# Attention and a SwiGLU FFN on one core: the result tiles of an output group dealt out differently, and two batches of VectorE work issued one instruction per TensorE step

## The chip, the cores and the metric

The kernel runs on one core of a Trainium2 chip. The metric is the device time of one execution in microseconds; the median of three runs of the kernel before is 1584.55 us. Engines are called as the profile calls them: PE (TensorE matmul), PEld (its weight loads), DVE (VectorE), ACT (ScalarE), POOL (GpSimd), SP (the queue that issues the DMAs).

## The reference

```python
# q, k, v: (8, 12, 448, 64) float32
q_n, k_n = rmsnorm(q, g_q), rmsnorm(k, g_k)
scores = q_n @ k_n.T / sqrt(64)                    # per sequence and head
attn = exp(scores - max) / (sum + 1e-9)
x = (attn @ v) as (B*S, H*D)                       # (3584, 768)
xn = x / rms(x) * rms_g
g = xn @ w_gate;  val = xn @ w_val                 # (768, 1536) each
out = (silu(g) * val) @ w_out                      # (1536, 768)
```

## The kernel before

Eight sequences (b = 0 to 7) of 448 tokens go through two halves. The attention half works in 48 groups g of two heads; six groups make a sequence. The FFN half of earlier sequences is laid between the attention's matmuls as a list of small **steps**: in the steady part, while the attention of one sequence runs, the gate and value products of the sequence before it run, and the output projection of the one before that. Everything is float32.

The order is written out by hand. `pe(fn)` emits one step of PE work, counts a clock `now["t"]` by one, and then emits whatever `after(n, ...)` has made due at that count, in the order in which it was asked for. `fill()` takes FFN steps from the list `todo`, calls `pe` for each, and behind each may emit one small DVE job more. An engine runs its own instructions in the order of emission; between engines, semaphores hold an instruction until its data, and the place it writes, are ready. A pool with a few buffers gives them out in the order in which they were released.

**Gate and value products.** `quad(b, fp)` (fp = 0 to 5) works out one block with seven half-size products (`p1`, `p6`, `p2`, `p7`, `p5`, `p4`, `p3_last`). `product` is line 1000. The result of `p1` is copied by ACT from its PSUM bank to the SBUF tile `p1` (line 1044), since `p2` goes on adding onto that same bank. The partial sums u2, u3, c21 and cc are DVE adds (line 1012) into single-buffer tiles of these names. `hand` (lines 1019 to 1023) makes h = silu(gate) * value.

**Output projection in quads.** For b = 2, 3, 5, 6, 7 (`in_quads`) the output projection is `out_quads`: a Strassen scheme within a Strassen scheme. There are seven groups i = 0 to 6 (`ORDER_Q`: B11, B21, T2, T3, T4, T1, B22), each of four steps: `a`, `bb`, `c` (12 PE records each) and `d` (6 records), with `d(i)` emitted after `a(i + 1)`. All their matmuls are line 1296. `c(i)` ends in one DVE add out of its bank (line 1328); `d(i)` accumulates onto one half of the same bank and so waits for that add; its own add is line 1335. `left_q1` (line 1171) makes the left operands of group i+1 by three DVE instructions within `c(i)`, and a fourth within `bb`. A group's result sits in two 128x384 places `dst[i]`, given by `rows(name)`: some in tiles of the `quad` code (p1, c21, u2, u3, cc), some in output tiles y. `finish(i)` combines groups on POOL (line 1268): after T1 it adds T1 onto `dst[3]`, then T2 (`dst[2]`) onto T1; after B22, the last group, it adds T1 (`dst[5]`) onto B22.

**The two seams.** Where a quad projection ends, the first product `p1` of the next gate block is emitted ahead of the last `d(6)`, and its ACT copy is put one step later, behind `d(6)`. I call this the **closing seam**; it exists at b = 3, 4, 6, 7.

Where a gate block ends and its output projection begins is the **opening seam**. Count steps from `p3_last` of fp = 5 as step 0. Step 1 is `norm_x` of the next sequence (a PE transposition that spreads 1/rms; for the last sequence an empty step), then come `a(0)`, `bb(0)`, `c(0)`, `a(1)`, `d(0)`, `bb(1)`, `c(1)`, `a(2)`, `d(1)`, `bb(2)` and so on, with attention steps between in most places. Into these steps fall three batches of DVE work:

- six scalings of x (`scale`, line 663, in place), two each at steps 1, 2 and 3;
- two times four **left sums** of the outer scheme (`left_sums`, lines 1148 to 1151), four at step 3 and four at step 4; the first group that reads one is i = 2;
- four sums of the scaled x (`op`, line 680, the list `slow`), one behind each FFN step once three steps have gone by since `norm_x`, if the group's attention steps are four steps back. `p1` of the next block empties what is left.

Of the kernel before, what the change touches and what calls it, by code (L numbers as in the profile page):

```python
# [8 lines left out]
F32 = mybir.dt.float32  # L9
# [3 lines left out]
ALU = mybir.AluOpType  # L13
# [5 lines left out]
B, H, S, D = 8, 12, 448, 64  # L19
# [3 lines left out]
NPAIR = H // 2  # L23
NDC, NFC = DM // 128, DF // 128
HALF = DM // 2
BW = 384
# [309 lines left out]
def safe_scores(  # L336
# [20 lines left out]
    nc = tc.nc  # L357
# [7 lines left out]
    e_pool, tmp, y_pool, rest_pool = pool("c_e", 11), pool("c_tmp", 1), pool("c_y", 3), pool("c_rest", 2)  # L365
# [8 lines left out]
    st = {}  # L374


    now, due = {"t": 0}, []

    def after(n, fn):
        due.append((now["t"] + n, fn))  # L380
# [6 lines left out]
            item[1]()  # L387


    NG = B * NPAIR  # L390


# [258 lines left out]
    def norm_x(b):  # L651


        rs = st.pop(("rx", b))
        ps = (ps_s if b else ps_f).tile([128, 512], F32, name="rb", tag="s" if b else "f")
        for t in range(NT):
            nc.tensor.transpose(ps[:, t * P:(t + 1) * P], rs[:, t:t + 1].to_broadcast([P, 128]), ident[0:P, 0:P])

        xs = [st["x", b, h] for h in range(2)]

        def scale(hp):
            x = xs[hp // 3][:, hp % 3, :]
            nc.vector.scalar_tensor_tensor(x, x, rg[:, hp:hp + 1], ps[:, 0:S], ALU.mult, ALU.mult)  # L663

        for hp in range(NPAIR):
            if b:
                after(hp // 2, lambda hp=hp: scale(hp))
            else:
                scale(hp)
        if b == 0:  # L670
            return

        a = st["left", b] = {f"A{r + 1}{h + 1}": xs[h][:, :, r * HT:(r + 1) * HT] for r in range(2) for h in range(2)}
        for h in range(2):
            st.pop(("x", b, h))

        def op(name, first, second, what):

            a[name] = a["A21"] if name == "S3" else s_pool.tile([128, 3, HT], F32, name="xs")
            nc.vector.tensor_tensor(a[name], a[first], a[second], what)  # L680

        slow.extend(lambda args=args: op(*args) for args in (("S1", "A21", "A22", ALU.add), ("S2", "S1", "A11", ALU.subtract),
                                                             ("S3", "A11", "A21", ALU.subtract), ("S4", "A12", "S2", ALU.subtract)))
        st["x_at"] = now["t"]

    slow = []

    def hurry():
        while slow:
            slow.pop(0)()  # L690

    NFP = NFC // 2

# [80 lines left out]
    for fc in range(NFC):  # L774
        col, fp = divmod(fc, NFP)
# [66 lines left out]
    def in_quads(b):  # L842
        return b > 1 and len(out_pairs(b)) == 2
# [161 lines left out]
    def quad(b, fp):  # L1005

        bank, add = {}, {}
        shift = 64 * (b % 2)

        def plus(name, ps, other, dst=None):  # L1010
            add[name] = tmp.tile([128, S], F32, name=name, tag=name, bufs=1) if dst is None else dst
            nc.vector.tensor_tensor(add[name], ps[:, 0:S], add[other], ALU.add)  # L1012

        def hand(gate, value, dst):

            th = tmp.tile([128, S], F32, name="th", tag="th", bufs=2)
            n = gate.shape[-1] * (gate.shape[1] if len(gate.shape) == 3 else 1)
            th = th[:, 0:n] if len(gate.shape) == 2 else th.rearrange("p (r n) -> p r n", r=2)
            nc.scalar.activation(th, gate, ACT.Tanh, scale=0.5)  # L1019

            def rest():
                nc.vector.scalar_tensor_tensor(dst, th, 1.0, gate, ALU.add, ALU.mult)
                nc.vector.scalar_tensor_tensor(dst, dst, 0.5, value, ALU.mult, ALU.mult)

            after(1, rest)

        def rows(fc):
            return h_of(fc)[:, shift:shift + S]

        def p1():  # L1030
            if fp == 0:
                hurry()
            if fp < 2:

                for g in (fp, fp + 2):
                    if carries(b - 1):
                        nc.gpsimd.tensor_copy(carried[g], group(out_pairs(b - 1)[-1][1] + 1, g))
                    if b % 2:
                        nc.gpsimd.tensor_copy(hs[g][:, :, 0:64], hs[g][:, :, S - 64:S])
            bank["a"] = product(b, fp, "A11", "B11")  # L1040

            def copy():
                add["p1"] = tmp.tile([128, S], F32, name="p1", tag="p1", bufs=1)
                nc.scalar.copy(add["p1"], bank["a"][:, 0:S])  # L1044

            if fp == 0 and in_quads(b - 1):
                after(1, copy)
            else:
                copy()

        def p6():
            bank["b"] = product(b, fp, "S2", "T2")
            plus("u2", bank["b"], "p1")

        def p2():
            product(b, fp, "A12", "B21", onto=bank["a"])
            hand(bank["a"][:, 0:HT], bank["a"][:, HT:S], rows(fp)[:, 0:HT])

        def p7():
            bank["c"] = product(b, fp, "S3", "T3")  # L1060
            plus("u3", bank["c"], "u2")

        def p5():
            bank["e"] = product(b, fp, "S1", "T1")
            add["cc"] = tmp.tile([128, 2, S], F32, name="cc", tag="cc", bufs=1)
            plus("c22", bank["e"], "u3", dst=add["cc"][:, 1, :])

        def p4():
            bank["d"] = product(b, fp, "A22", "T4")
            plus("c21", bank["d"], "u3")  # L1070
            after(1, lambda: hand(add["c21"][:, 0:HT], add["c21"][:, HT:S], rows(fp)[:, HT:S]))

        def p3():
            product(b, fp, "S4", "B22", onto=bank["e"])
            plus("c12", bank["e"], "u2", dst=add["cc"][:, 0, :])
            after(1, lambda: hand(add["cc"][:, :, 0:HT], add["cc"][:, :, HT:S], rows(fp + NFP).rearrange("p (r n) -> p r n", r=2)))

        def sums(n):

            st["left_sums"] = now["t"]  # L1080
            half = fp // KG
            if n < len(out_pairs(b)):
                left_sums(b, n, half)

        def p3_last():
            if fp == NFP - 1 and in_quads(b):
                after(1, lambda: left_q1(b, 0, range(3)))
            p3()
            if fp % KG == KG - 1:
                after(3, lambda: sums(0))  # L1090
                after(4 if fp == NFP - 1 else 5, lambda: sums(1))

        return [p1, p6, p2, p7, p5, p4, p3_last]

    OUT_PARTS = 3
# [45 lines left out]
    def left_sums(b, n, half):  # L1141

        pair, row = (0, n) if in_quads(b) else (n, 0)
        if half == 0:
            for i, name in enumerate(("S1", "S2", "S4")):
                st["so", b, pair, row, name] = room_so[3 * n + i].rearrange("p (c n) -> p c n", c=NFP)
        of = lambda name: left_group(b, pair, name, row, half)
        nc.vector.tensor_tensor(of("S1"), of("A21"), of("A22"), ALU.add)
        nc.vector.tensor_tensor(of("S2"), of("S1"), of("A11"), ALU.subtract)
        nc.vector.tensor_tensor(of("S3"), of("A11"), of("A21"), ALU.subtract)  # L1150
        nc.vector.tensor_tensor(of("S4"), of("A12"), of("S2"), ALU.subtract)

    def left_o(b, pair, name, c):
        return left_group(b, pair, name, 0, c // KG)[:, c % KG, :]
# [88 lines left out]
    def out_quads(b):  # L1243

        bank, dst, steps = {}, {}, []
# [5 lines left out]
        def rows(name):  # L1251

            if name in ("B11", "T1"):
                return [tmp.tile([128, S], F32, name=t, tag=t, bufs=1)[:, 0:BW] for t in ("p1", "c21")]
            if name == "T3":
                u3 = tmp.tile([128, 2, S], F32, name="cc", tag="cc", bufs=1)
                return [u3[:, row, 0:BW] for row in range(2)]
            if name == "T2":
                return [tmp.tile([128, S], F32, name=t, tag=t, bufs=1)[:, 0:BW] for t in ("u2", "u3")]
            return [y_pool.tile([128, HALF], F32, name="y", tag="y") for _ in range(2)]  # L1260

        def out(what, n, first):
# [62 lines left out]
        def c(i):  # L1325
            ps = two(i, "c")
            u3 = st["u", b, i][:, 1:2].to_broadcast([128, 2, HW])
            nc.vector.tensor_tensor(dst[i][1].rearrange("p (h n) -> p h n", h=2), ps, u3, ALU.add)  # L1328
            if i + 1 < len(ORDER_Q):
                left_q1(b, i + 1, range(3))  # L1330

# [63 lines left out]
    def fill(n=None):  # L1395
# [8 lines left out]
        for _ in range(min(n, len(todo))):  # L1404
# [10 lines left out]
            pe(fn)  # L1415
            convert()

            if slow and now["t"] - st["block"] > 4 and now["t"] - st["x_at"] > NPAIR // 2:
                slow.pop(0)()
            if now["t"] - st["block"] > 4 and now["t"] != st.get("left_sums"):  # L1420
                left = 3 - sum(derive() for _ in range(3))
# [77 lines left out]
        for _ in range(n):  # L1499
            convert()  # L1500


    def at_once(steps):
        for step in steps:
            step()

    at_once(squares(0, 0))
    warm(9)
# [1 line left out]
    scale = norm_rests(0, 0, 2)  # L1510
    steps = squares(0, 1)
# [11 lines left out]
    for g in range(NG + 1):  # L1523
        b, hp = divmod(g, NPAIR)
# [124 lines left out]
```

## Time and profile before

| | |
|---|---|
| median of 3 runs | 1584.55 us (1583.27 to 1585.42) |
| the profiled execution: its own time | 1584.46 us |
| its span, first to last instruction | 1582.7 us |
| PE busy | 1546.3 us, 98% of the span |
| DVE busy | 978.9 us, 62% |
| POOL busy | 723.8 us, 46% |
| ACT busy | 473.3 us, 30% |
| mean granted PE clock | 0.995 |
| opening seams, start of `a(0)` | about 624, 818, 1182, 1373 and 1523 us |
| closing seams, end of the last group | about 694, 888, 1254 and 1432 us |

A row of a group or of the timeline reads: start, duration, engine, line and operation, output from input as partitions x elements, the number of instructions, and in brackets the idle time ahead of it with the instruction that ended it. A PE row counts hardware records, two for each matmul in the code. In the table of waits the three numbers are the total, the number of times and the longest, in us.

### The profile page before, as it was taken

To read this page: it belongs to the slowest core of one execution; us is meant where nothing else is said; L and a number is where in the kernel's file an instruction comes from. 1 tells how busy PE (TensorE), PEld (TensorE's weight loads), DVE (VectorE), ACT (ScalarE), POOL (GpSimd) and SP (SyncE) were. 2 spreads that over 40 slices of the span, in tenths; PEclk is the share of its full clock that TensorE was granted. 3 is DMA by queue.
4 is the path that set the end of the run, shared out by engine and by line. 5 is a ranking of instruction groups with operands and counts; after the bars stand their busy time and mean duration, and the time that the engine had idled before them with its cause. 6 is when DMAs were issued, how large, how long until landed. Compare 5 with 4: busy or idle time off the path is not lost.

```text
span 1582.7 us, 23667 instructions
## 1 busy us (share of the span) xinstructions
PE 1546.3 (98%) x7916; PEld 1195.9 (76%) x7916; DVE 978.9 (62%) x1697; ACT 473.3 (30%) x955; POOL 723.8 (46%) x718
## 2 busy tenths in 40 slices
PE   8999999999999999999999999999999999999997
PEld 4344445787756888788878888667887788899997
DVE  6889898669754666854567444534658545563454
ACT  6746464232222222223222222323322222101000
POOL 6867877454324443564335652444544541021003
PEclk9999999999999999999999999999999999999998
DMA  7648574866789979785547854584557744578565
GB/s 209 211 144 265 165 242 138 264 215 214 246 274 290 316 221 300 225 259 154 160 141 243 250 158 140 154 265 131 160 152 224 232 143 143 159 246 259 174 194 185
DMA packets 313414, 327.10 MB, mean 207 GB/s; under 512 B 83652, under 2 KB 310212, under 8 KB 313284
## 3 DMA queue, kind: packets, MB, share of 16 engines
q1 hardware_dynamic: 312356, 325.30, 66.6%
q8 instruction: 65, 1.06, 0.3%
q14 instruction: 65, 0.53, 0.1%
q10 hardware_dynamic: 800, 0.20, 0.1%
q0 software_dynamic: 128, 0.00, 0.0%
HBM read 271.62 MB, written 53.77 MB: 206 GB/s over the span
## 4 chain that ended last, share of the span: by engine, by line
PE 72%; DVE 12%; issue 1%; POOL 1%; DMA 1%; ACT 0%; SPq 0%; DVEq 0%; POOLq 0%
PE ff L1000 40%; PE ff L1296 9%; PE ff L1228 5%; PE sc L545 5%; PE av L597 5%; PE ff L1104 2%; PE sc L575 2%; DVE l L1171 2%; PE den L610 2%; PE tr L527 1%; DVE rd L618 1%; DVE x L663 1%; DVE top L768 1%; DVE top L769 1%; DVE ms L487 0%
## 5 line engine op out<-in xcount | busy, mean ns | idle before, releaser
L1000 PE MATMUL ff<-x,w 128*128 128x224 f32 x1866 | 380.9, 354 | 4.0 <-ACT p L1044 4.0
L1000 PEld LDWEIGHTS ff<-x,w 128*128 128x128 f32 x1866 | 348.2, 190 | 20.8 <-issue 11.1
L555 POOL TENSOR_TENSOR es<-e 128x448 f32<-128x448 f32 x82 | 93.1, 1156 | 437.3 <-ACT e L549 437.3
L1000 PE MATMUL ff<-xs,w 128*128 128x224 f32 x1392 | 284.6, 353 | 3.2 <-DVE w L922 2.9
L1000 PEld LDWEIGHTS ff<-xs,w 128*128 128x128 f32 x1392 | 261.9, 190 | 4.9 <-issue 4.1
L562 POOL TENSOR_TENSOR es<-es,e 64x448 f32<-64x448 f32 (+1 forms) x164 | 196.4, 1208 | 6.3
L618 DVE RECIPROCAL rd<-rd 128x448 f32<-128x448 f32 x41 | 121.0, 2951 | 94.4 <-ACT rd L617 94.4
L549 ACT ACTIVATE e<-sc,rs 128x448 f32<-128x448 f32 x288 | 161.5, 635 | 49.8 <-PE sc L545 47.4
L545 PE MATMUL sc<-qT,kT 64*128 64x448 f32 x576 | 138.0, 572 | 1.9 <-ACT e L549 0.7
L597 PE MATMUL av<-e,vt 128*64 128x448 f32 x576 | 118.8, 548 | 0.0
L506 POOL TENSOR_TENSOR rs<-ms,mhalf 128x12 f32<-128x12 f32 (+1 forms) x50 | 115.9, 2318 | 4.2
L545 PEld LDWEIGHTS sc<-qT,kT 64*128 64x128 f32 x576 | 54.0, 185 | 82.5 <-issue 68.5
L1296 PE MATMUL ff<-w,l 128*128 128x192 f32 x578 | 110.9, 332 | 4.7 <-DVE c L1328 3.6
L1012 DVE TENSOR_TENSOR cc<-ff,u 128x448 f32<-128x448 f32 x84 | 52.4, 624 | 100.9 <-PE ff L1000 100.8
L1361 PE MATMUL ff<-x,w 128*128 128x448 f32 x288 | 111.8, 542 | 0.0
L1296 PEld LDWEIGHTS ff<-w,l 128*128 128x128 f32 x578 | 97.5, 193 | 8.7 <-DVE c L1328 4.2
L597 PEld LDWEIGHTS av<-e,vt 128*64 128x64 f32 x576 | 37.1, 136 | 75.6 <-issue 74.8
L1361 PEld LDWEIGHTS ff<-x,w 128*128 128x128 f32 x288 | 53.3, 190 | 50.7 <-issue 48.9
L1019 ACT ACTIVATE th<-c 128x224 f32<-128x224 f32 x42 | 16.3, 389 | 227.1 <-DVE c L1012 227.1
L1268 POOL TENSOR_TENSOR y<-y,p 128x384 f32<-128x384 f32 x10 | 11.6, 1160 | 154.4 <-DVE y L1335 150.3
L631 POOL TENSOR_TENSOR ss<-ss,rd 128x448 f32<-128x448 f32 x40 | 46.4, 1159 | 77.2 <-ACT rd L630 77.2
L809 POOL TENSOR_TENSOR w<-top,raw 128x384 int32<-128x384 int32 x63 | 66.4, 1068 | 25.9 <-issue 8.4
(201 smaller groups left out, 2335.0 us busy)
## 6 DMA issues: line engine op xcount, KB each, us to landing
w<-kept SPq DMA_DIRECT2D x512, 192.0 KB, 3.5
w<-kept_q SPq DMA_DIRECT2D x323, 192.0 KB, 3.5
w<-kept_o SPq DMA_DIRECT2D x136, 192.0 KB, 3.8
kept<-w SPq DMA_DIRECT2D x91, 192.0 KB, 3.7
kept_q<-w SPq DMA_DIRECT2D x57, 192.0 KB, 3.2
qk<-in_q_dram SPq DMA_DIRECT2D x48, 192.0 KB, 3.7
qk<-in_k_dram SPq DMA_DIRECT2D x96, 96.0 KB, 3.6
vt<-in_v_dram SPq DMA_DIRECT2D x48, 192.0 KB, 3.5
```

Of the source, the lines that this page charges most:

```text
L506: nc.gpsimd.tensor_tensor(st["rs", g][:, cols], ms, mhalf[:, cols], ALU.pow)
L545: nc.tensor.matmul(ps[:, 0:S], lhsT=kT[r, c * 128:(c + 1) * 128], rhs=qT[r, :], start=True, stop=True)
L549: nc.scalar.activation(e, ps[:, 0:S], ACT.Exp, scale=rs[:, n:n + 1])
L555: nc.gpsimd.tensor_tensor(es, st["e", g, 0, j], st["e", g, 1, j], ALU.add)
L562: nc.gpsimd.tensor_tensor(es[r], es[r], e[r], ALU.add)
L597: nc.tensor.matmul(av[own(j), 0:S], lhsT=vt[:, j, c], rhs=st["e", g, c, j], start=False, stop=(c == NK - 1), skip_group_check=True)
L618: nc.vector.reciprocal(rd, rd)
L809: nc.gpsimd.tensor_tensor(data(key).bitcast(I32), top, lo, ALU.add)
L1000: nc.tensor.matmul(bank[:, w * HT:(w + 1) * HT], lhsT=wt[:, c * 128:(c + 1) * 128], rhs=x[:, c, :], start=onto is None and w == c == 0, st ...
L1228: nc.tensor.matmul(ps, lhsT=left_o(b, which, LEFT_O[name], c), rhs=data(("wo", b, name, c)), start=first and c == 0, stop=c == NFP - 1, sk ...
L1296: nc.tensor.matmul(ps, lhsT=a[:, j, :], rhs=data(key)[:, n % 2 * HW:(n % 2 + 1) * HW], start=start and j == 0, stop=j == KG - 1, skip_grou ...
L1361: nc.tensor.matmul(bank[w][:, 0:S], lhsT=data(key)[:, c * 128:(c + 1) * 128], rhs=st["x", 0, half][:, c, :], start=half == c == 0, stop=ha ...
```

## The change

Five edits:

1. **Places.** `rows` gives groups B11 and T1 the tiles (c21, u3) in place of (p1, c21), and T2 the tiles (p1, u2) in place of (u2, u3).
2. **The copy of p1** is emitted within `p1` everywhere; the special case that moved it behind `d(6)` is gone.
3. **Left sums.** For quad blocks the second half's eight sums are put on a list `first_sums` at step 3. `fill` emits one behind each FFN step, and `c(1)` empties the list before it makes the left operands of group 2. For other blocks, all sums of the last fp come at step 3.
4. **Scaling of x** goes one per step, at steps 1 to 6.
5. **The sums of x** (`slow`) begin once six steps have gone by since `norm_x`, and only when `first_sums` is empty.

```diff
             if b:
-                after(hp // 2, lambda hp=hp: scale(hp))
+                after(hp, lambda hp=hp: scale(hp))
...
-    slow = []
-
-    def hurry():
-        while slow:
-            slow.pop(0)()
+    slow, first_sums = [], []
+
+    def hurry(jobs):
+        while jobs:
+            jobs.pop(0)()
...
             bank["a"] = product(b, fp, "A11", "B11")
-
-            def copy():
-                add["p1"] = tmp.tile([128, S], F32, name="p1", tag="p1", bufs=1)
-                nc.scalar.copy(add["p1"], bank["a"][:, 0:S])
-
-            if fp == 0 and in_quads(b - 1):
-                after(1, copy)
-            else:
-                copy()
+            add["p1"] = tmp.tile([128, S], F32, name="p1", tag="p1", bufs=1)
+            nc.scalar.copy(add["p1"], bank["a"][:, 0:S])
...
                 after(3, lambda: sums(0))
-                after(4 if fp == NFP - 1 else 5, lambda: sums(1))
+                after(3 if fp == NFP - 1 else 5, lambda: sums(1))
...
-        nc.vector.tensor_tensor(of("S1"), of("A21"), of("A22"), ALU.add)
-        nc.vector.tensor_tensor(of("S2"), of("S1"), of("A11"), ALU.subtract)
-        nc.vector.tensor_tensor(of("S3"), of("A11"), of("A21"), ALU.subtract)
-        nc.vector.tensor_tensor(of("S4"), of("A12"), of("S2"), ALU.subtract)
+        ops = [lambda args=args: nc.vector.tensor_tensor(*(of(name) for name in args[:3]), args[3])
+               for args in (("S1", "A21", "A22", ALU.add), ("S2", "S1", "A11", ALU.subtract),
+                            ("S3", "A11", "A21", ALU.subtract), ("S4", "A12", "S2", ALU.subtract))]
+        if half and in_quads(b):
+            first_sums.extend(ops)
+        else:
+            at_once(ops)
...
             if name in ("B11", "T1"):
-                return [tmp.tile([128, S], F32, name=t, tag=t, bufs=1)[:, 0:BW] for t in ("p1", "c21")]
+                return [tmp.tile([128, S], F32, name=t, tag=t, bufs=1)[:, 0:BW] for t in ("c21", "u3")]
...
             if name == "T2":
-                return [tmp.tile([128, S], F32, name=t, tag=t, bufs=1)[:, 0:BW] for t in ("u2", "u3")]
+                return [tmp.tile([128, S], F32, name=t, tag=t, bufs=1)[:, 0:BW] for t in ("p1", "u2")]
...
             nc.vector.tensor_tensor(dst[i][1].rearrange("p (h n) -> p h n", h=2), ps, u3, ALU.add)
+            if i == 1:
+                hurry(first_sums)
...
-            if slow and now["t"] - st["block"] > 4 and now["t"] - st["x_at"] > NPAIR // 2:
+            if first_sums:
+                first_sums.pop(0)()
+            elif slow and now["t"] - st["block"] > 4 and now["t"] - st["x_at"] >= NPAIR:
                 slow.pop(0)()
```

`at_once(steps)` calls each of its steps in turn; it is only moved up in the file. `NPAIR` is 6.

## The prediction

> **What bounds the kernel now.** I read the busy shares first, then PE's table of waits, then the timeline at each wait.
>
> ```profile
> PE 1546.3 (98%) x7916; PEld 1195.9 (76%) x7916; DVE 978.9 (62%) x1697; ACT 473.3 (30%) x955; POOL 723.8 (46%) x718
> ```
>
> PE sets the time: 36.4 us of its span are idle, and the change neither adds nor removes an instruction on any engine. It can only fill PE's gaps or open new ones. Which gaps it can reach, the table of waits tells:
>
> ```profile
> PE ff L1000 <- ACT p L1044: 4.0, 3, 1.7
> PE ff L1296 <- DVE c L1328: 3.6, 2, 3.4
> ...
> PE ff L1296 <- DVE p L1335: 2.0, 3, 0.7
> ```
>
> The first line lies at three closing seams (1.41, 0.84 and 1.74 us), the second at two opening seams, the third at the other three (0.68 us each). The closing seam at 1254 us:
>
> ```profile
> 1249.64 1.00 POOL L1268 TENSOR_TENSOR p<-p,u 128x384 f32<-128x384 f32 x1
> ...
> 1252.45 1.00 POOL L1268 TENSOR_TENSOR y<-y,p 128x384 f32<-128x384 f32 x1
> 1253.40 1.00 POOL L1268 TENSOR_TENSOR y<-y,c 128x384 f32<-128x384 f32 x1
> 1253.48 0.53 ACT L1044 COPY p<-ff 128x448 f32<-128x448 f32 x1 [12.12 <-POOL y L1268]
> 1254.06 2.54 PE L1000 MATMUL ff<-x,w 128*128 128x224 f32 x12 [1.74 <-ACT p L1044]
> ```
>
> See that tile p1 is still the result of T1: the copy stands until POOL's second-to-last add has read it, though p1's product was finished at 1249.1. PE finished p6 at 1252.3 and stood for p2.
>
> The opening seam at 1373 us, where no attention step lies between:
>
> ```profile
> 1381.98 0.55 DVE L1151 TENSOR_TENSOR raw<-top,raw 128x384 f32<-128x384 f32 x1
> 1382.45 1.27 DVE L663 SCALAR_TENSOR_TENSOR x<-x,rg,rb 128x448 f32<-128x448 f32 x2
> 1383.63 0.55 DVE L1328 TENSOR_TENSOR c<-ff,th 128x384 f32<-128x384 f32 x1
> 1384.10 0.55 DVE L1171 TENSOR_TENSOR l<-h,h 128x384 f32<-128x384 f32 x1
> 1384.24 4.21 PE L1296 MATMUL ff<-w,l 128*128 128x192 f32 x12 [3.37 <-DVE c L1328]
> ```
>
> DVE has no gap here: c(0)'s add, for a bank that PE had filled by 1378.75, comes behind four left sums and two scalings. And the wait costs more than its length. The stretches after it (columns: length, then busy time and records of PE, PEld, DVE, ACT and POOL, clock, DMA share, GB/s):
>
> ```profile
> 1384.24:1388.24 4.00, 4.00 (x13) 4.00 (x13) 3.93 (x9) 0.00 (x0) 0.00 (x0) 0.50 0.28 88
> 1388.24:1392.18 3.94, 3.94 (x19) 3.94 (x19) 3.27 (x7) 0.00 (x0) 0.00 (x0) 0.74 0.55 164
> 1392.18:1400.00 7.82, 7.82 (x51) 7.82 (x50) 5.53 (x13) 0.32 (x1) 1.95 (x2) 1.00 0.52 155
> ```
>
> PE is granted half its clock for 4 us and 0.74 for another 4: 30 records (d(0), bb(1), c(1)) take 7.94 us. At full clock 12 records take 1.96 us (the a(2) of the last seam, 1536.90 to 1538.86), so 30 take 4.9. **3.1 us** are lost to the clock on top of 3.37.
>
> At the opening seams with attention between, the reader is to see DVE's backlog delay the reciprocal, which had its input at 831.4 (ACT's copy from 830.86, 0.53 us):
>
> ```profile
> 834.22 2.94 DVE L618 RECIPROCAL rd<-rd 128x448 f32<-128x448 f32 x1
> ...
> 837.80 0.35 DVE L1335 TENSOR_TENSOR p<-ff,th 128x192 f32<-128x192 f32 x1
> ...
> 838.21 2.22 PE L1296 MATMUL ff<-w,raw 128*128 128x192 f32 x12 [0.68 <-DVE p L1335]
> ```
>
> **What the Trainium skill says.** "TensorE: Matmul & The Clock Gate", Part 1, "What's actually happening", says that PE falls to half clock after an idle window of about 3.4 us, on a free-running window, and returns after about as long a busy one. The trace agrees: 3.37 us idle, then 0.50; the 1.74 us wait at 1254 left no such mark. The same page ("Architectural detail") says that ACT and DVE are strictly first in, first out; so c(0)'s add can't pass the sums. "SBUF — State Buffer", "SBUF: two separate sides", says that a DVE instruction with two SBUF inputs and a POOL instruction lock each other out. The sums of x of line 680 agree: 0.85 us mostly, up to 1.79.
>
> **Part 1: places and copy (edits 1 and 2).** p1 becomes the first place of T2, and T2 is last read by POOL's third add after T1, not by the adds after B22. At 1254 that third add starts at 1249.64 and ends at 1250.64; the copy then runs 1250.7 to 1251.2, and PE reaches p2 at 1252.33: no wait. The other two seams: third add ends 691.84 and 885.94, copy done 692.4 and 886.5, PE at p2 at 693.5 and 887.6. The cover is p6 (2.4 us of PE); slack is 1.1 us each. The fourth seam (1432) has no wait. What is late next: the u2 add waits for the fourth add (1251.6), before p6's end; u3, now in T1, is read until POOL's last add ends (1254.4), and is written after p7, which follows p2. At the opening, c21 is now written by a(0); its earlier readers are `hand`'s two DVE instructions, queued ahead on DVE anyway: nothing. The copy now heads ACT's queue some 1.5 us early; ACT was idle for 9 to 12 us there, so nobody stands behind it. **Gain 4.0 us**, bounds 3.0 and 4.2.
>
> **Part 2: the opening seam at 1373 (edits 3 to 5).** In backlog DVE's instructions follow at: scaling 0.59, left sum 0.50, half-width add 0.27, full add 0.47, two `hand` instructions 1.19, bb's two adds and left operand 1.13, three left operands 1.53 (differences of starts in the timeline). From 1375.50, in the new order: scaling, a(0)'s add, scaling, hand: 1378.15; bb(0): 1379.27; scaling 1379.86; one sum 1380.36; c(0)'s add ends 1380.9. PE ends a(1) at 1380.86: wait **0.1 instead of 3.37**, and the clock stays full, 3.1 more. Given back: by c(1) five sums are out, so it emits three sums ahead of group 2's left operands. Carrying the queue on (left operands, scaling, sum, half add; scaling, sum, half add; scaling, sum; bb(1), sum): c(1)'s add runs 1387.8 to 1388.35, d(1) could start at 1387.8: wait 0.55. Then three sums and two left operands end at 1390.95, against d(1)'s end at 1389.4: bb(2) waits 1.6. The sums of x follow after, and PE needs nothing of them. 3.37 + 3.07 - 0.1 - 0.55 - 1.6 = **4.2 us**, bounds 1 (the clock drops again) and 6.4 (no wait comes back).
>
> **Part 3: the three seams with attention.** From 820.36 the queue loses three of six scalings and three of four sums ahead of c(0)'s add, and ahead of the reciprocal five of eight sums and one sum of x (1.5): it empties by 830.3, the reciprocal starts at 831.45, d(0)'s add at 835.0 instead of 837.8. The 0.68 goes. At c(1) the six instructions end left operand S2 at about 840.6; PE, past a(2), d(1) and a transposition, needs it at 841.0. The scaling that ends last holds its PSUM bank until 830.3; the third score matmul, which takes it, comes at about 831.4. **Gain 3 x 0.68 = 2.0 us**, bounds 0 and 3.3 (another 0.4 each near 848, where a weight load of L1296 waits for a left operand).
>
> **Part 4: the last seam (1523).** No scaling; waits of 0.22 and 0.52 go, bb(2) waits some 0.4 for the three sums: **gain 0.4**, bounds -0.5 and 1. At the openings of b = 1 and 4 four sums may move up a step and scalings move back; their first reader is eight steps off and PE has no DVE wait on them there: nothing.
>
> **Sum**: 4.0 + 4.2 + 2.0 + 0.4 = 10.6. The profiled execution took 1584.46 (span 1582.7 and 1.8 around it): 1573.9; the median stands 0.09 above it: **1574.0 us**. 0.2% is 3.2 us, about what a measurement can tell from no change.
>
> **Rivals.**
> A (0.15): *the clock falls again at 1388*. Two waits of 0.55 and 1.6 us lie within 3.2 us. For it: the window is free-running. Against: PE works 1 us between them. Gain 10.6 - 3.1 = 7.5: 1577.
> B (0.09): *the gaps are refilled*: the weights' transfers become the bound. For: DMA engines are 0.67 busy on average. Against: PE waits for a DMA once, 1.8 us, at the start. It, or an order that doesn't come out as I read it, gives 1582 to 1584.5.
> C (0.07): *slower*, by the bunch at c(1). If POOL locks DVE out (line 1171 took 1.48 instead of 0.55 at 876.70 beside POOL's sums), six instructions take 8.4 instead of 3.1 us, bb(2) waits over 3.4 us and the clock halves: 3 x (3.4 + 3.1) = 19.5 at the attention seams, against 8.6 gained elsewhere: 1595. It decides from a wait of 3.4 us on. Against: POOL is idle from 837.5 to 842.1, just there.
> My forecast has 0.69.
>
> **How the numbers follow.** The forecast's own parts span 1570.5 (upper bounds of parts 2 and 3, halved) to 1577; with A up to 1579; 1580 leaves out B, C and a little below. Faster 0.84 (forecast and A), same 0.09, slower 0.07.
>
> **What would show it.** In the table of waits, L1000 <- ACT L1044 gone; L1296 <- DVE c L1328 below 0.5, clock 1.00 throughout; a new wait of 1 to 2 us on L1171 near 1381 (b = 6's bb(2)); reciprocals right after ACT's copy; POOL and ACT busy times unchanged. Wrong if waits on line 1171 or 1000 for DMA total over 4 us, or if the clock shows 0.5 at bb(2).

## The result and the profile after

The median fell from 1584.05 us to **1576.3 us** (six runs each; the 1584.55 given above is of the first three), by 7.75 us. The ratio is 0.9952, 95% interval [0.9939, 0.9965]. The profiled execution took 1576.27 us with a span of 1574.4, 8.3 less than before. The forecast was 1574.0, in a range of 1570.5 to 1580.0: the direction and the range held, the gain was 7.75 where the sum had 10.6.

The changed kernel's line numbers differ: L1004 is L1000 of before, L1046 is L1044, L614 is L610, L667 is L663, L684 is L680; the left sums are L1145, d's add is L1337.

PE's table of waits, of the changed kernel (total, times, longest; lines that the change doesn't touch left out):

```profile
PE ff L1004 <- DVE w L926: 2.9, 2, 1.5
PE ff L1296 <- DVE l L1171: 2.8, 8, 1.2
...
PE den L614 <- DVE x L667: 0.9, 1, 0.9
...
PE ff L1296 <- DVE u L1328: 0.5, 1, 0.5
```

The first line was there before. The 4.0 us on ACT's copy are gone, and so are the 3.6 and 2.0 us on DVE's adds L1328 and L1335. Three waits are new: left operands (L1171), a scaling (L667), and a c add later in the scheme (L1328, at c(2)).

The closing seam, 1254 us before, in the changed kernel's timeline:

```profile
1247.79 1.00 POOL L1268 TENSOR_TENSOR c<-c,p 128x384 f32<-128x384 f32 x1
1248.74 1.00 POOL L1268 TENSOR_TENSOR u<-u,u 128x384 f32<-128x384 f32 x1
1248.82 0.53 ACT L1046 COPY p<-ff 128x448 f32<-128x448 f32 x1 [9.32 <-POOL c L1268]
...
1250.31 2.43 PE L1004 MATMUL ff<-x,w 128*128 128x224 f32 x12
1250.60 0.99 POOL L1268 TENSOR_TENSOR y<-y,c 128x384 f32<-128x384 f32 x1
```

The copy goes when POOL's third add has read p1, and p2 starts without a bracket, before POOL has even begun the adds after B22.

The opening seam of b = 6, in the changed kernel's timeline:

```profile
1375.41 0.67 DVE L667 SCALAR_TENSOR_TENSOR x<-x,rg,rb 128x448 f32<-128x448 f32 x1
...
1376.00 0.55 DVE L1145 TENSOR_TENSOR raw<-h,h 128x384 f32<-128x384 f32 x1
1376.47 0.55 DVE L1328 TENSOR_TENSOR u<-ff,th 128x384 f32<-128x384 f32 x1
...
1377.07 2.30 PE L1296 MATMUL ff<-w,l 128*128 128x192 f32 x12
...
1386.23 0.56 DVE L1171 TENSOR_TENSOR l<-l,raw 128x384 f32<-128x384 f32 x1
...
1386.84 1.24 PE L1296 MATMUL ff<-w,l 128*128 128x192 f32 x6 [1.22 <-DVE l L1171]
```

Behind bb(0)'s instructions only one scaling and one left sum stand ahead of c(0)'s add (two scalings and four sums before); d(0) starts with no wait. Nine microseconds later bb(2) waits 1.22 us for its left operand, behind the three sums that c(1) emits. The clock is 1.00 throughout (same columns as in the prediction):

```profile
1376.64:1380.64 4.00, 3.93 (x24) 3.53 (x23) 3.96 (x9) 0.32 (x1) 0.00 (x0) 1.00 0.87 278
1380.64:1384.64 4.00, 3.87 (x24) 3.58 (x23) 3.97 (x10) 0.31 (x1) 0.00 (x0) 1.00 0.95 309
1384.64:1388.64 4.00, 2.78 (x17) 2.48 (x17) 3.96 (x9) 0.01 (x1) 0.00 (x0) 1.00 0.17 54
```

To see where the 8.3 us went, I took the starts of the same PE instructions in both timelines: `norm_x` (rb), the `p1` behind each quad projection, the last seam's `a(0)`. Lengths of the stretches between them, in us:

| stretch | before | after | difference |
|---|---|---|---|
| start to norm_x of b = 1 (which opens b = 0) | 248.66 | 248.65 | 0.0 |
| that opening, to the next norm_x | 177.20 | 178.28 | **+1.08** |
| openings of b = 2, 3, 5, norm_x to p1 | 64.59, 64.57, 64.58 | 64.54 each | -0.12 together |
| closings, p1 to the next norm_x, b = 3, 4, 6 | 129.52, 128.95, 125.86 | 127.84, 127.84, 123.85 | -1.68, -1.11, -2.01 |
| opening of b = 6, norm_x to p1 | 53.81 | 50.35 | **-3.46** |
| closing at b = 7, p1 to the last a(0) | 96.46 | 96.32 | -0.14 |
| opening of b = 7, to the last step | 49.13 | 48.24 | -0.89 |

All other stretches agree within 0.01; what follows the last step of PE is 0.08 longer. The sum is -8.3. I use such stretches below beside the medians, since the first 250 us varied by up to 2.1 us from one profile to the next without a change in their code (248.65 to 250.79), and what follows the last step by up to 1.4 us.

### The profile page after: what moved, and what is told of

Its sections match the earlier page's. It is cut to its first block, busy times and chain, and to the rows that moved or that the text cites. A ratio compares the mean times of both kernels' runs of the same rounds, so it can differ in the third digit from the quotient of the medians.

```text
span 1574.4 us, 23664 instructions
## 1 busy us (share of the span) xinstructions
PE 1544.4 (98%) x7916; PEld 1193.3 (76%) x7916; DVE 979.7 (62%) x1697; ACT 472.7 (30%) x955; POOL 724.0 (46%) x718
## 3 DMA queue, kind: packets, MB, share of 16 engines
HBM read 271.62 MB, written 53.77 MB: 207 GB/s over the span
## 4 chain that ended last, share of the span: by engine, by line
PE 75%; DVE 9%; issue 1%; DMA 1%; POOL 0%; ACT 0%; SPq 0%; DVEq 0%; POOLq 0%; ACTq 0%
PE ff L1004 42%; PE ff L1296 10%; PE sc L549 6%; PE av L601 5%; PE ff L1228 5%; PE sc L579 2%; PE den L614 2%; PE ff L1101 2%; PE tr L531 1%; DVE l L1171 1%; DVE top L772 1%; DVE rd L622 1%; DVE top L773 1%; DVE top L771 1%; DVE xs L684 1%
## 5 line engine op out<-in xcount | busy, mean ns | idle before, releaser
L1004 PE MATMUL ff<-x,w 128*128 128x224 f32 x1866 | 380.4, 354 | 0.0
L1004 PEld LDWEIGHTS ff<-x,w 128*128 128x128 f32 x1866 | 348.5, 190 | 15.6 <-issue 11.1
L1004 PE MATMUL ff<-xs,w 128*128 128x224 f32 x1392 | 284.6, 353 | 3.2 <-DVE w L926 2.9
L1004 PEld LDWEIGHTS ff<-xs,w 128*128 128x128 f32 x1392 | 261.9, 190 | 4.9 <-issue 4.1
L1296 PE MATMUL ff<-w,l 128*128 128x192 f32 x578 | 110.0, 329 | 3.7 <-DVE l L1171 2.6
L1296 PEld LDWEIGHTS ff<-w,l 128*128 128x128 f32 x578 | 95.4, 190 | 9.7 <-DVE l L1171 4.5
L1268 POOL TENSOR_TENSOR y<-y,c 128x384 f32<-128x384 f32 x10 | 12.2, 1216 | 151.9 <-DVE y L1337 143.0
```

The lines of the kernel that those rows point to most:

```text
L1004: nc.tensor.matmul(bank[:, w * HT:(w + 1) * HT], lhsT=wt[:, c * 128:(c + 1) * 128], rhs=x[:, c, :], start=onto is None and w == c == 0, st ...
L1296: nc.tensor.matmul(ps, lhsT=a[:, j, :], rhs=data(key)[:, n % 2 * HW:(n % 2 + 1) * HW], start=start and j == 0, stop=j == KG - 1, skip_grou ...
```

## The experiments

My account after the result: four separate mechanisms, namely tile p1 at the closings, DVE's order at the opening of b = 6 with PE's clock in it, a gain at the attention seams that DVE's backlog takes back one group later, and a PSUM bank held by the scalings at the opening of b = 0. The rivals are named in each expectation.

**e1: places and copy alone (edits 1 and 2 on the kernel before).** Its edit is the `p1` part and the two `rows` parts of the diff under "The change".

> The kernel before with edits 1 and 2 alone. If the closing seams are a wait for tile p1 and nothing else, the three waits of L1000 on ACT's copy go and the rest of the trace stays: 4.0 us by the waits of before, 4.8 us by what the landmarks of the changed kernel show (1.67 + 1.11 + 2.01); 1579.3 us. If the gain there came from the openings (a DVE less in arrears at the end of the quads), the waits stay at 4.0 us and the time at 1584.

Measured: 1579.77 us against 1584.09, ratio 0.997 [0.996, 0.998]. The closings took 127.84, 127.84 and 123.85 us, exactly as in the changed kernel; openings of b = 2, 3 and 5 stayed at 64.6. So edits 1 and 2 account for the closings, without the DVE edits. Which of the two carries it was not separated: new places with the copy still behind `d(6)` were not run. The other half, the early copy with T1 still in p1, is no test: it would come ahead of the adds that still read the tile.

Its opening of b = 6 held a surprise: 52.05 us where before had 53.81, with nothing changed there. Its wait and the stretches around it (its L1289 and L1321 are L1296 and L1328 of before):

```profile
PE ff L1289 <- DVE u L1321: 3.4, 1, 3.4
```

```profile
1375.97:1379.97 4.00, 0.63 (x5) 0.34 (x4) 3.97 (x9) 0.32 (x1) 0.00 (x0) 1.00 0.59 190
1379.97:1383.97 4.00, 3.48 (x21) 3.08 (x21) 3.93 (x9) 0.00 (x0) 0.00 (x0) 1.00 0.50 148
```

PE waits the same 3.4 us for the same add, and the clock does not fall: 21 records in the next 4 us instead of 13. But this is one execution. Its mean clock was 0.998; six of e1's nine executions had 0.994 to 0.996, so in most of them the clock probably fell.

**e2: two scalings per step at the opening of b = 0.**

```diff
-                after(hp, lambda hp=hp: scale(hp))
+                after(hp // 2 if b == 1 else hp, lambda hp=hp: scale(hp))
```

> The changed kernel, but at the opening of b = 0 (norm_x of sequence 1) the scalings go two per step as before. If the 1.1 us that the changed kernel lost at 262 us is the denominators' PSUM bank, held until the last scaling, the wait of L614 on L667 goes and the time falls by 1.1 us, to 1575.2. If the 1.1 us are a chance of that one profile, nothing changes: 1576.3.

Measured: 1575.27 us, ratio to before 0.9949 [0.9935, 0.9962]. By its interval this is not apart from the changed kernel; the stretch decides. The opening of b = 0 takes 177.19 us again, and the wait of L614 on L667 is gone. In the changed kernel it reads

```profile
260.68 1.27 DVE L667 SCALAR_TENSOR_TENSOR x<-x,rg,rb 128x448 f32<-128x448 f32 x2
...
262.10 0.97 PE L614 MATMUL den<-es,ones 128*64 128x448 f32 x4 [0.88 <-DVE x L667]
```

The transposed 1/rms sits in a bank of the scores' pool until the last scaling has read it. At this opening few FFN steps lie before the attention, and weight conversions share DVE's queue, so the denominators' matmul comes to that bank before the scaling is done.

**e3, e11, e12: PE's clock at the opening of b = 6.** e3 is the kernel before with PE kept busy through the wait; e11 and e12 are the kernel before itself.

```diff
             ps = bank[i, "c"]
+            if b == 6 and i == 0:
+                warm(14)
             term(i, 6, ps[:, 1], start=False)
```

> The kernel before, with 14 matmuls of the identity into a spare PSUM bank ahead of d(0) at the opening of b = 6 (their result is not used). They take 3.3 us, as long as PE waits there for DVE, so they add work and remove no wait. If the half clock after the wait is lost time, the clock stays at 1.00 and the time falls: by up to 3.1 us, but DVE is in arrears and gives part back at bb(2), about 1.8 us by its queue: 1582.2. If DVE alone sets that stretch, the clock is full and the time is the same, 1584, or later by what the matmuls run over.

> The kernel before, unchanged, profiled once more, for the clock at the opening of b = 6. If half clock follows whenever PE waits 3.4 us, the stretch from norm_x to the next p1 takes 53.8 us again with a clock of 0.50 in it. If it hangs on where the wait falls against a window that runs on its own, it can take 52.05 us with the clock at 1.00, as in e1, where the wait was 3.37 us too.

> The kernel before, a third profile, for the same question: 53.8 us with the clock fallen, or 52.05 us with a full clock, at the same wait of 3.4 us.

Measured: e3 took 1583.05 us (0.9998 [0.9989, 1.0006]: by time, undecided), and its opening 52.05 us at full clock. e11 took 1584.46 us, opening 53.77; e12 1585.55 us, opening 52.52, with the same wait of 3.4 us in both. In e3 all 13 executions had a mean clock of 0.997 or 0.998; the kernel before had 0.995 or 0.996 in 18 of 69.

So a wait of 3.4 us may cost the clock for 6.8 us (before, e11), for 3.4 us (e12), or not at all (the profile of e1, whose opening is not changed). The traces of these four profiles show on what it hangs. Here are the stretches between the moments at which the clock can change, for before, e12 and e1 (columns as above):

```profile
1380.07:1383.48 3.41, 0.80 (x5) 0.50 (x4) 3.38 (x7) 0.32 (x1) 0.00 (x0) 1.00 0.91 299
1383.48:1386.89 3.41, 2.65 (x8) 2.65 (x9) 3.34 (x8) 0.00 (x0) 0.00 (x0) 0.50 0.04 6
1386.89:1390.30 3.41, 3.41 (x12) 3.41 (x12) 2.88 (x6) 0.00 (x0) 0.00 (x0) 0.50 0.60 179
1390.31:1393.72 3.41, 3.41 (x23) 3.41 (x22) 3.25 (x7) 0.00 (x0) 0.00 (x0) 1.00 0.75 231
```

```profile
1382.90:1386.31 3.41, 0.29 (x2) 0.29 (x3) 3.41 (x7) 0.15 (x1) 0.00 (x0) 1.00 0.53 177
1386.31:1389.72 3.41, 3.41 (x12) 3.41 (x12) 3.34 (x9) 0.00 (x0) 0.00 (x0) 0.50 0.33 94
1389.72:1393.13 3.41, 3.41 (x22) 3.41 (x22) 3.38 (x8) 0.00 (x0) 0.00 (x0) 1.00 0.73 218
```

```profile
1374.74:1378.15 3.41, 1.59 (x10) 1.29 (x8) 3.34 (x9) 0.32 (x1) 0.00 (x0) 1.00 0.90 290
1378.15:1381.56 3.41, 1.86 (x11) 1.75 (x12) 3.38 (x7) 0.00 (x0) 0.00 (x0) 1.00 0.11 40
```

The moments lie on a grid. Before, the clock falls at 1383.48, returns at 1390.31 and falls once more behind the last matmul, at 1574.62: 2 and 54 times 3.413 us (e11 falls at 1383.51 and returns at 1390.33). In e12 it is 1386.31, 1389.72 and 1577.46: 1 and 55 times. In e1 the clock falls only at the end, at 1569.30, and its grid is counted back from there: 56 times 3.413 us before it lies 1378.15, in the middle of the wait (1376.33 to 1379.70). The same wait, nearly whole within one stretch, leaves PE 0.80 or 0.29 us of work there, and the clock falls; split over two, it leaves 1.59 and 1.86 us, and the clock stays. Once halved, the clock came back behind a stretch of 3.41 us of work, not behind one of 2.65. That fits a window that runs on its own ("TensorE: Matmul & The Clock Gate", Part 1, "What's actually happening", which puts its length at about 3.4 us). How little work is too little is not settled: behind the last matmul the clock also fell after stretches with up to 1.66 us of work (e6).

The two openings also price the fall: 53.81 - 52.05 = **1.76 us** for two halved stretches, and 52.52 - 52.05 = 0.47 for one, though 30 records had taken 3.1 us longer in the first case. Part of the rest shows as a wait that the profile of before does not have, PE at full speed waiting for DVE's next add, here in e1 (e3 has it too, also 0.52):

```profile
1383.49 0.92 PE L1289 MATMUL ff<-w,h 128*128 128x192 f32 x4 [0.52 <-DVE y L1309]
```

e3 alone proves little, since e1 kept its clock with PE idle; together they show that idle PE and busy PE at full clock cost the same 52.05 us. DVE sets that stretch. The 1.76 us belong to the profile compared: an execution of the kernel before in which the wait falls otherwise on the grid has less to gain.

**e4: sums of x from the 20th step on.**

```diff
-            elif slow and now["t"] - st["block"] > 4 and now["t"] - st["x_at"] >= NPAIR:
+            elif slow and now["t"] - st["block"] > 4 and now["t"] - st["x_at"] >= 20:
```

> The changed kernel, with the sums of x (L684) begun 20 steps after norm_x instead of 6. If the gain of 0.85 us at the attention seams is given back because DVE, with sums of x beside POOL's adds (one of 1.78 us), is late with group 3's left operands, b3's wait goes at three seams: 0.6 us each, and about 0.5 us at c(2) of b = 6: 1574.0 in all. If the left operands are late for another reason, or the late sums only move the wait to a later group, 1576.3.

Measured: 1576.53 us, as the changed kernel. The stretches say why: openings of b = 2, 3 and 5 fell to 63.67, 63.64 and 63.65 (0.9 each), b = 6 to 49.50, but the opening of b = 0 grew by 1.28 us and that of b = 4, with what follows to the next norm_x, from 171.17 to 172.40: two waits of L1004 on L684 (1.0 us each), where few steps are left and `p1` has to run the sums itself. The mechanism at the attention seams is confirmed, the remedy was too wide. What DVE does there in the changed kernel:

```profile
844.25 1.78 DVE L684 TENSOR_TENSOR xs<-xs,x 128x672 f32<-128x672 f32 x1
845.96 0.55 DVE L1328 TENSOR_TENSOR u<-ff,th 128x384 f32<-128x384 f32 x1
846.43 1.01 DVE L1171 TENSOR_TENSOR l<-h,h 128x384 f32<-128x384 f32 x1
847.48 0.56 DVE L1171 TENSOR_TENSOR l<-l,h 128x384 f32<-128x384 f32 x1
```

A sum of x, 1.78 us instead of 0.85 beside POOL's adds, stands ahead of the operands that bb(3) waits for until 848.09. The kernel before has such a sum in nearly the same place (1.79 us at 844.96): DVE was no earlier there before the change, PE was only too late to wait for it.

**e5 and e6: edit 3 alone, and edits 4 and 5 alone, on the kernel before.**

```diff
 # e5 (ops: the four left sums, and hurry with a list, as in the change)
-                after(4 if fp == NFP - 1 else 5, lambda: sums(1))
+                after(3 if fp == NFP - 1 else 5, lambda: sums(1))
...
+        if half and in_quads(b):
+            first_sums.extend(ops)
...
+            if i == 1:
+                hurry(first_sums)
...
-            if slow and now["t"] - st["block"] > 4 and now["t"] - st["x_at"] > NPAIR // 2:
+            if first_sums:
+                first_sums.pop(0)()
+            elif slow and now["t"] - st["block"] > 4 and now["t"] - st["x_at"] > NPAIR // 2:
 # e6
-                after(hp // 2, lambda hp=hp: scale(hp))
+                after(hp, lambda hp=hp: scale(hp))
...
-            if slow and now["t"] - st["block"] > 4 and now["t"] - st["x_at"] > NPAIR // 2:
+            if slow and now["t"] - st["block"] > 4 and now["t"] - st["x_at"] >= NPAIR:
```

> The kernel before with edit 3 alone (left sums one per step, scalings two per step, places as before). By DVE's queue the wait for c(0)'s add at the opening of b = 6 falls from 3.4 to about 1.9 us. If half the clock is granted only after a wait of some 3.4 us, the clock stays full and the seam gains 1.5 + 3.1 less some 1.7 given back at bb(2), with 0.9 at the last seam and no loss at 262 us: 1580.3. If the clock falls after a wait of 1.9 us too, 1583.4.

> The kernel before with edits 4 and 5 alone (scalings one per step, sums of x from the sixth step on). The wait for c(0)'s add falls from 3.4 to about 1.6 us. Full clock: 1.8 + 3.1 less some 1.4 given back, and 1.1 lost at 262 us: 1581.6. If edits 3 and 4 add up as parts of one wait, e5 and e6 together gain what the changed kernel gains at the openings (3.4 us); if the clock is a step, each alone takes most of it and their sum is larger than that, some 6 us.

Measured: e5 1582.08 us against 1584.46 (0.9987 [0.9981, 0.9994]), between its two expectations; e6 **1586.34** (1.0012 [1.0005, 1.0019]), slower. At b = 6 the wait for c(0)'s add fell to 1.8 and 1.6 us, the clock stayed at 1.00, and the stretch took 50.70 and 50.53 us. Against 52.05 without a clock loss that is 1.35 and 1.52; both together give 1.70. They share one wait, as I expected, but e6's sign I had wrong: its openings of b = 2, 3 and 5 are 65.56 to 65.58, **1.0 us longer** each, beside the 1.1 at b = 0. Within the whole change edit 3 makes up for that 1.0. Edits 4 and 5 were not run apart, but at each of these three seams e6 has a wait that neither before nor the changed kernel has, here at b = 3:

```profile
835.18 1.02 PE L545 MATMUL sc<-qT,kT 64*128 64x448 f32 x2 [0.43 <-DVE x L663]
```

A score matmul waits for the last scaling: a bank of the scores' pool again, as at b = 0, and so a cost of edit 4. Behind it comes a wait of 0.5 us for c(2)'s add (line 1328), which stands behind a sum of x of 1.78 us; that edit 5 has a part in this wait is not shown.

**e7: left sums in the order of need, the list emptied at c(2).**

```diff
-            if i == 1:
+            if i == 2:
                 hurry(first_sums)
...
+            if row == 1:
+                first_sums[:] = [first_sums[k] for k in (0, 1, 4, 5, 2, 6, 3, 7)]
```

> The changed kernel, with the left sums in the order in which groups read them (S1 and S2 of both rows first), and the list emptied at c(2) instead of c(1). If the bunch of three sums at c(1) makes bb(2) wait, its waits on L1171 (1.2 us at b = 6, 0.2 at the other seams) go, and up to half comes back one group later: 1575.0, between 1574.4 and 1576.0. If the bunch is not the cause, 1576.3.

Measured: **1573.3 us**, ratio to before 0.9924 [0.991, 0.9937], better than expected. b = 6 opens in 48.09 us (from 50.35), the attention seams in 63.79 to 63.82 (from 64.54), the last in 47.78 (from 48.24). The waits on L1171 fall from 2.8 us to 0.8. By the stretches e7 gains some 5 us on the changed kernel, by the medians 3.0; the first 250 us, which vary, took 2.1 us longer in its profile. The bunch at c(1) was the cause. The new order and the later emptying were not tried one by one.

**e8, e9, e10: the remedies together.** e8 is e2, e4 and e7 in one. e9 is e8 with the late sums of x only where a quad block opens; e10 is e9 with two scalings per step everywhere.

```diff
 # e9, against e8
         st["x_at"] = now["t"]
+        st["x_wait"] = 20 if in_quads(b - 1) else NPAIR
...
-            elif slow and now["t"] - st["block"] > 4 and now["t"] - st["x_at"] >= 20:
+            elif slow and now["t"] - st["block"] > 4 and now["t"] - st["x_at"] >= st["x_wait"]:
 # e10, against e9
-                after(hp // 2 if b == 1 else hp, lambda hp=hp: scale(hp))
+                after(hp // 2, lambda hp=hp: scale(hp))
```

> The changed kernel with all three: two scalings per step at the opening of b = 0, sums of x from 20 steps on, left sums by need. If the three losses are separate waits, their gains add up: 1.1 + 2.3 + 1.3, 1571.6. If the last two are one backlog of DVE, seen twice, about 1573.

> The kernel of e8, but the sums of x wait for 20 steps only where the block that opens is a quad block, and 6 steps elsewhere. In e8 the stretch from b = 0's opening to the next took 1.2 us longer than in e2 and the stretch after b = 4's opening 1.2 us longer than in the changed kernel, with PE waiting for L684 both times (1.9 us together). If those are sums left over for p1, they go: 1572.85 - 2.4 = 1570.4. If the late sums cost elsewhere too, 1572 to 1573.

> The kernel of e9, with the scalings of x two per step at every opening, as before the change. If the left sums carry the gain at the openings and one scaling per step is worth only 0.35 us at b = 6 (50.70 us with edit 3 alone, 50.35 with all), 0.3 us slower than e9: 1570.7. If scalings ahead of c(0)'s add delay the attention seams too, 0.5 to 1 us at three seams: 1572.5.

Measured: e8 1572.85 us (0.9925 [0.9911, 0.9938]); e9 **1569.33** (0.9903 [0.9887, 0.992]), the lowest median; e10 1570.49 (0.9911 [0.9894, 0.9927]). The intervals overlap, so I go by the stretches. In e8 the attention seams fall to 63.23, 0.4 below e4 and 0.6 below e7: 1.31 gained where 0.89 and 0.75 were gained singly. At b = 6 it takes 48.10, as e7 alone. So it is in part one backlog of DVE, relieved at two points. e9 takes back the 1.2 us at b = 0 and at b = 4 (177.19 and 171.16 us). e10's attention seams are e9's to 0.01 us; only b = 6 is longer, 49.40 against 48.10, with a wait of 1.8 us for c(0)'s add. So one scaling per step is worth 1.3 us at b = 6, where I had expected 0.3, and, with the other remedies in, nothing elsewhere.

## Why the prediction was right or wrong

- **Part 1, closings: right in mechanism, too low.** 4.0 forecast, with 4.2 as the upper bound; 1.68 + 1.11 + 2.01 = 4.80 measured, and 0.14 at the fourth seam. Each closing gained 0.27 us more than its row of waits showed (1.41, 0.84, 1.74). The row leaves out what a wait costs besides: without it p2 starts 0.16 us before p6's row ends (1250.31 against 1250.47), and its own 12 records take 2.43 us instead of 2.54.
- **Part 2, opening of b = 6: right in mechanism, its terms mis-sized.** 4.2 forecast, 3.46 measured. The wait for c(0)'s add went as computed. d(1) waited 0.13 us (0.55 computed) and bb(2) 1.22 (1.6 computed), 18.2 us after norm_x where my queue has 18.45; the "near 1381" of my list of signs does not follow from it. Then came 0.50 for c(2)'s add, which my queue had not reached. The term for the clock failed: 3.07 (my own figures give 3.04) was taken as PE's lost time; e1 and e3 price it at 1.76, and the profile of e1 shows that the fall need not come at all. The order of DVE's work by itself gained 1.70 where the other terms gave 1.1.
- **Part 3, attention seams: wrong.** 2.0 forecast, 0.12 measured. The step that failed is "The 0.68 goes" as a gain kept. The wait did go, the reciprocal and d(0)'s add came where I had them, and PE ran 0.84 us ahead at a(2) (838.21 before, 836.70 after, with 0.67 of lead brought along). But I followed DVE's queue only to bb(2). All four sums of x now lie behind the reciprocal, and bb(3) got its left operand at about the old time: it could start at 848.80 before and at 848.09 after, a lead of 0.71 again. I had even seen a weight load wait near 848 for that operand, and booked it as a further gain; it was the sign that DVE sets the pace there. e4 and e7 each give 0.75 to 0.9 of it back.
- **Part 4: half right.** The last seam gained 0.89 (0.4 forecast; bb(2) waited 0.19 instead of 0.4). Of the openings without quads I named b = 1 and 4, and these lost nothing (197.39 and 171.17 us in both). b = 0 I left out, a term put at nothing without a reason, and it lost 1.08. I had seen that the last scaling holds a bank of the scores' pool, and checked it only at the attention seams of quad blocks, where it is free in time as long as edit 3 thins the queue. e2 shows the loss, e6 what happens without edit 3.
- **Rivals.** A (the clock falls again at bb(2)) did not happen in that profile: 1.00. (By the grid, a wait of 1.6 us is short for it: waits of 1.6 and 1.8 us in e5, e6 and e10 left the clock at 1.00.) B did not either: PE's only wait for a DMA is the one at the start, 1.4 us. C had its place right, the bunch at c(1), but not its size: the attention seams waited 0.2 to 0.3 us on L1171 at a time, not 3.4.
- **The range.** Its lower end, 1570.5, takes the upper bounds of parts 2 and 3 whole (2.2 + 1.3 us), not halved as I wrote.

That the total came near is in part luck: the errors offset each other, +0.9 and +0.5 against -0.7, -1.9 and -1.1.

## What to carry to other kernels

When work on an engine in arrears is spread or moved, follow its queue until it is empty again, not just to the first wait that goes: the same instructions still have to run before the next operand. For each instruction that is put off, list the tile or bank that it is last to read, at every place where the pattern occurs; the cost turned up at the one opening that I had left out. And spread work in the order in which it is needed: the same eight sums, reordered and with one group more to come out in, were worth 3 us more by the medians (1573.3 against 1576.3) and 5 by the stretches.

## What was unexpected of the hardware

The clock of PE fell after a wait of 3.4 us in three profiles of the same kernel, for 6.8 us in two and 3.4 in one, and after the same wait in the profile of e1 not at all. What differs is where the wait lies on a grid of 3.413 us. The stretch between two of its points need not be idle throughout, as I had read it: 0.80 us of PE work in 3.41 did not keep the clock, while 2.65 us did not bring it back. It stayed at 1.00 after waits of 1.6 to 1.8 us in e5, e6 and e10.
